# Transposing one head pair's features ahead of three others, in the one block that gets them from SBUF

## The chip, the cores and the metric

The kernel runs on one core of a Trainium2 chip. A core has five engines with queues of their own: TensorE (PE in the profile, with PEld for its weight loads), VectorE (DVE), ScalarE (ACT), GpSimd (POOL) and SyncE (SP, which issues the DMAs here). Each engine takes its instructions in the order in which they stand; between engines they wait for each other by semaphores. The metric is the device time of one execution in microseconds, as the median of several runs.

## The reference

Four sequences of 576 tokens, 8 heads of 64 features. The result of attention goes through a two-layer block with a squared ReLU.

```python
scores = scale * q @ k^T, causal;  a = softmax(scores);  local = a @ v
phi(x) = where(x > 0, x, exp(x) - 1) + 1
mem_out = (phi(q) @ M_prev) / (phi(q) @ z_prev + 1e-6)
g = sigmoid(beta);  attn = g * mem_out + (1 - g) * local      # per head
x = attn as [2304 tokens, 512]
out = relu(x @ w_in)^2 @ w_out                                # 512 -> 2048 -> 512
```

All inputs and the result are float32.

## The kernel before

*Tiling.* Heads are worked on in 4 pairs a sequence, each pair filling the 128 partitions. A sequence's first 64 tokens are computed in `first_tokens`, apart from the others; the remaining 512 tokens are four query tiles of 128. For the first two sequences a pair is done in two passes, tiles 1 and 2 of all pairs first and then tiles 3 and 4; for the last two, all four tiles at once. The two-layer block works on blocks of 256 tokens: block 0 holds the first 64 tokens of all four sequences, block 1 the tiles 1 and 2 of sequence 0, and so on to block 8.

*Attention.* `attention` loads the pair's `kd`, `qm` and `vv`, splits them into a high and a low part (`qh`, `ql` on L363 and L364, `kh`, `kl`; the low parts repair the precision of a faster kind of matmul), computes scores into a PSUM tile `sp` of two banks with one buffer (L466), lets DVE add the mask and take the row's extreme while it copies them to SBUF (L485), exponentiates on ACT (L505), makes two float16 parts `a`, transposes them by DMA (`aT`, L549) and multiplies with the split values `vs` (L570 to L575). `memx` holds the pair's part of the memory term (L443), to which the local term is added (L585); a tile pair's features are then written to the DRAM tensor `xd` (L596). One pair's are kept back: those of the last pair of sequence 0 for tiles 1 and 2, which go into the list `last` as the SBUF tile `memx`.

*The two-layer block.* `moe(n)` makes eight groups `up` (L653 to L655: 24 matmuls of 256 columns each), squares and splits them (`r`, `gh`, `gl`), and adds them into `oacc` (L643 to L645: 12 matmuls of 512 columns for each group). After its seventh group, `prefetch` fetches the next block's features: a load `xn` from `xd` (L617), transposes on PE into a PSUM tile `px` (L620, L622), a copy `xh` on ACT (L625) and the rest `xl` on DVE (L626), all twice, for 128 tokens each. `px` and `up` share two PSUM buffers. Block 1 alone gets the list `last` as `tail`: three quarters of its features are read from `xd`, and the last quarter is transposed straight from `memx`.

*What sets the order.* `merge` interleaves the steps of attention, of the weights' loading and of block 0 in program order. From that, the framework's scheduler makes each engine's queue when the kernel is built: it plays the program through with a timing model and takes, whenever an engine is free in it, the ready instruction that stands first. So moving one instruction can reorder what comes after it on all engines. PSUM has two buffers each for `up`, `oacc` and for the small tiles `av` (`acc`, `pm`, `vt`), and the two banks of `sp`.

Of the kernel before, what the change touches and what calls it, by code (L numbers as in the profile page):

```python
# [8 lines left out]
F32 = mybir.dt.float32  # L9
# [81 lines left out]
def fused_kernel(ctx: ExitStack, tc: tile.TileContext, t0_d, zt_d, kk_d, qv_d, beta, w_in, w_out, out):  # L91
    nc = tc.nc
# [8 lines left out]
    ident = identr.bitcast(F32)  # L101
# [508 lines left out]
    def prefetch(b, blk, tail=None):  # L610
        nk = NK if tail is None else NK - 1
        xh = mo.tile([P, NK, BLK], F32R, tag="xh", name="xh", bufs=2)
        xl = mo.tile([P, NK, BLK], F32R, tag="xl", name="xl", bufs=2)
        for t in range(2):
            r0 = QT[1 + 2 * blk + t][0]
            src = mo.tile([P, DM], F32R, tag="x", name="xn", bufs=XB)
            nc.sync.dma_start(src.bitcast(F32)[:, : nk * P], xd[b][r0 : r0 + P, : nk * P])  # L617
            px = ps.tile([P, NK, P], F32R, tag="up", name="px", bufs=2)
            for k in range(nk):
                nc.tensor.transpose(px[:, k], src[:, k * P : (k + 1) * P], identr)  # L620
            if tail is not None:
                nc.tensor.transpose(px.bitcast(F32)[:, nk], tail[:, t], ident)  # L622
            px = px.bitcast(F32)
            ts = slice(t * P, (t + 1) * P)
            nc.scalar.copy(xh[:, :, ts], px)  # L625
            nc.vector.tensor_tensor(out=xl[:, :, ts], in0=px, in1=xh[:, :, ts].bitcast(F32), op=ALU.subtract)  # L626
        return xh, xl

    def moe(n):
# [17 lines left out]
        for j in range(NF // 2):  # L647
# [23 lines left out]
            if j == PJ and n + 1 < NBLK:  # L671
                assert n > 0 or last
                xq.append(prefetch(*blocks[n + 1], *last))
                last.clear()
                yield
# [133 lines left out]
```

## Time and profile before

| | |
|---|---|
| median of 3 runs | 601.41 us (599.22 to 602.59) |
| the profiled execution | 599.29 us |
| its span, first to last instruction | 597.5 us |
| PE busy | 551.6 us (92%) |
| DVE busy | 412.5 us (69%) |
| ACT busy | 328.1 us (55%) |
| mean granted clock of TensorE | 0.983 |

PE's 92% is a mean: from 160 us to the end of attention at about 440 us it is busy nearly all the time beside a DVE that is busy too, and from there to the end it works alone. A matmul's length in the timeline overlaps that of the next; what one costs PE is the distance of two starts. An idle time in brackets behind an instruction is that of its engine just before it, with what ended it.

### The profile page before, as it was taken

How to read it: one execution, taken by the hardware profiler on the slowest of the kernel's cores; microseconds unless marked ns; L12 is line 12 of the kernel's file. 1: busy time of each engine (PE TensorE's matmuls, PEld its weight loads, DVE VectorE, ACT ScalarE, POOL GpSimd, SP SyncE). 2: the span in 40 equal slices, each digit the busy share in tenths (PEclk: the TensorE clock that was granted, in tenths of full speed). 3: DMA queues.
4: the chain of work that ended last, by engine and by line, in shares of the span. 5: the costliest groups of instructions: out<-in, count | busy, mean ns of one | idle time of the engine just before them, and what ended most of it. 6: DMA issues, size and time to landing. Idle time of an engine off the chain costs nothing.

```text
span 597.5 us, 11549 instructions
## 1 busy us (share of the span) xinstructions
PE 551.6 (92%) x4198; PEld 483.4 (81%) x4198; DVE 412.5 (69%) x1285; ACT 328.1 (55%) x747; POOL 171.6 (29%) x139
## 2 busy tenths in 40 slices
PE   2478998699999899999999999999999999999997
PEld 2356886497888788888888888998889999999996
DVE  5999898789879799898697898988985101101100
ACT  3699786476756576776566555573553222213212
POOL 2502122033433233322332334214333211221221
PEclk9977999999999999999999999999999999999999
DMA  8957746757646566575663547555344000100000
GB/s 278 412 200 277 234 141 124 148 136 177 139 119 123 153 149 170 144 185 156 124 132 80 157 122 147 135 149 140 47 101 131 29 1 35 37 1 18 20 0 36
DMA packets 127576, 76.28 MB, mean 128 GB/s; under 512 B 99360, under 2 KB 112672, under 8 KB 127520
## 3 DMA queue, kind: packets, MB, share of 16 engines
q1 hardware_dynamic: 127520, 75.55, 47.8%
q8 instruction: 33, 0.54, 0.4%
q14 instruction: 23, 0.19, 0.1%
HBM read 42.63 MB, written 8.78 MB: 86 GB/s over the span
## 4 chain that ended last, share of the span: by engine, by line
PE 48%; DVE 25%; DMA 11%; ACT 8%; issue 5%; SPq 2%; POOL 1%; ACTq 0%; DVEq 0%
PE up L653 7%; PE up L655 7%; PE up L654 7%; PE oacc L643 7%; PE oacc L645 7%; PE oacc L644 7%; DVE a L545 5%; DMA vv<-in_qv_dram 4%; PE sp L466 3%; DMA aT<-a 3%; ACT e L505 3%; DVE e L485 3%; DVE memx L585 3%; DVE raw L165 2%; DVE w L169 1%
## 5 line engine op out<-in xcount | busy, mean ns | idle before, releaser
L653 PE MATMUL up<-xh,w 128*128 128x256 f32 x576 | 167.2, 290 | 2.9 <-ACT aF L525 2.8
L654 PE MATMUL up<-xl,w 128*128 128x256 f32 x576 | 166.3, 289 | 0.0
L655 PE MATMUL up<-xh,w 128*128 128x256 f32 x576 | 166.2, 289 | 0.0
L668 POOL TENSOR_TENSOR gl<-r,gh 128x512 fp32r<-128x512 f32 x72 | 97.0, 1348 | 206.9 <-DVE gh L667 127.4
L653 PEld LDWEIGHTS up<-xh,w 128*128 128x128 f32 x576 | 111.9, 194 | 8.3 <-ACT aF L525 3.0
L643 PE MATMUL oacc<-w,gh 128*128 128x512 f32 x288 | 115.1, 400 | 0.3 <-DVE gh L667 0.3
L654 PEld LDWEIGHTS up<-xl,w 128*128 128x128 f32 x576 | 111.9, 194 | 3.2 <-issue 0.7
L644 PE MATMUL oacc<-w,gh 128*128 128x512 f32 x288 | 113.6, 394 | 0.0
L655 PEld LDWEIGHTS up<-xh,w 128*128 128x128 f32 x576 | 111.8, 194 | 1.5 <-issue 0.4
L505 ACT ACTIVATE e<-e,mx 128x320 f32<-128x320 f32 (+3 forms) x128 | 77.9, 609 | 62.9 <-DVE memx L585 33.0
L645 PE MATMUL oacc<-w,gl 128*128 128x512 f32 x288 | 109.1, 393 | 0.0
L659 ACT ACTIVATE r<-up 128x512 f32<-128x512 f32 x72 | 42.3, 588 | 115.9 <-PE up L655 103.9
L661 POOL TENSOR_TENSOR r<-r 128x512 f32<-128x512 f32 x40 | 49.1, 1229 | 153.3 <-ACT r L659 150.0
L667 DVE CAST gh<-r 128x512 fp32r<-128x512 f32 x40 | 16.9, 423 | 106.5 <-ACT r L663 102.8
L545 DVE SCALAR_TENSOR_TENSOR a<-e,a 128x128 f16<-128x128 f32 x120 | 75.7, 655 | 16.9 <-ACT a L543 16.7
L643 PEld LDWEIGHTS oacc<-w,gh 128*128 128x128 f32 x288 | 54.3, 189 | 9.5 <-DVE gh L667 0.5
L645 PEld LDWEIGHTS oacc<-w,gl 128*128 128x128 f32 x288 | 53.2, 188 | 10.3
L644 PEld LDWEIGHTS oacc<-w,gh 128*128 128x128 f32 x288 | 54.4, 189 | 8.5
L543 ACT ACTIVATE a<-e 128x128 f16<-128x128 f32 x120 | 55.8, 520 | 3.0 <-DMA aT<-a 2.1
L485 DVE CUSTOM_DVE_ANT_0 e<-sp,mask 128x320 f32<-128x320 f32 (+3 forms) x128 | 47.3, 414 | 0.3
L585 DVE SCALAR_TENSOR_TENSOR memx<-s,sm,memx 128x64 f32<-128x64 f32 x120 | 38.0, 357 | 1.4
L575 PE MATMUL acc<-vs,aT 128*128 128x128 f16 x308 | 36.9, 220 | 0.0
(127 smaller groups left out, 875.6 us busy)
## 6 DMA issues: line engine op xcount, KB each, us to landing
raw<-in_w_in_dram SPq DMA_DIRECT2D x11, 512.0 KB, 7.1
vv<-in_qv_dram SPq DMA_DIRECT2D x16, 320.0 KB, 3.3
raw<-in_w_out_dram SPq DMA_DIRECT2D x9, 512.0 KB, 7.2
kd<-in_kk_dram SPq DMA_DIRECT2D x16, 288.0 KB, 3.0
out_dram<-o SPq DMA_DIRECT2D x16, 256.0 KB, 2.0
xd<-memx SPq DMA_DIRECT2D x31, 128.0 KB, 1.9
xn<-xd SPq DMA_DIRECT2D x14, 256.0 KB, 2.7
qm<-in_qv_dram SPq DMA_DIRECT2D x8, 321.0 KB, 3.1
```

The lines of the kernel that those rows point to most:

```text
L485: nc.vector.tensor_tensor_reduce(out=e[:, h, ka:kb], in0=sps[:, h, cs], in1=mask[:, 448 - q0 + ka : 448 - q0 + kb], scale=-0.125, scalar=3 ...
L505: ex = nc.scalar.activation(e[:n, h, :ke], e[:n, h, :ke], AF.Exp, bias=bs, scale=-1.0, accum_out=sm[:n, h : h + 1])
L543: nc.scalar.mul(av[:, :, o0 : o0 + w], x, SC)
L545: nc.vector.scalar_tensor_tensor(out=av[:, :, o0 + w : o0 + 2 * w], in0=x, scalar=SC, in1=av[:, :, o0 : o0 + w], op0=ALU.mult, op1=ALU.sub ...
L585: nc.vector.scalar_tensor_tensor(out=xo, in0=s3[:n, h], scalar=sm[:n, h : h + 1], in1=xo, op0=ALU.mult, op1=ALU.add,)
L643: nc.tensor.matmul(acc[t], gh[:, u, ts], w_out_op(f, 0), start=f == 0, stop=False)
L644: nc.tensor.matmul(acc[t], gh[:, u, ts], w_out_op(f, 1), start=False, stop=False)
L645: nc.tensor.matmul(acc[t], gl[:, u, ts], w_out_op(f, 0), start=False, stop=f == NF - 1)
L653: nc.tensor.matmul(up[:, u, :], w_in_op(f, k, 0), xh[:, k, :], start=k == 0, stop=False)
L654: nc.tensor.matmul(up[:, u, :], w_in_op(f, k, 0), xl[:, k, :], start=False, stop=False)
L655: nc.tensor.matmul(up[:, u, :], w_in_op(f, k, 1), xh[:, k, :], start=False, stop=k == NK - 1)
L668: nc.gpsimd.tensor_tensor(out=gl, in0=r, in1=gh.bitcast(F32), op=ALU.subtract)
```

## The change

In `prefetch`, the transpose of the tail's quarter stands ahead of the loop over the quarters from `xd`, not behind it. Only block 1 has a tail, so only there do instructions trade places in the program.

```diff
             px = ps.tile([P, NK, P], F32R, tag="up", name="px", bufs=2)
+            if tail is not None:
+                nc.tensor.transpose(px.bitcast(F32)[:, nk], tail[:, t], ident)
             for k in range(nk):
                 nc.tensor.transpose(px[:, k], src[:, k * P : (k + 1) * P], identr)
-            if tail is not None:
-                nc.tensor.transpose(px.bitcast(F32)[:, nk], tail[:, t], ident)
```

The line numbers trade places too: the tail's transpose is L622 before and L620 after, the loop's L620 before and L622 after. Scheduled anew, PE's queue differs from the 321st to about the 3,100th of some 4,390 rows, and the other engines' queues over the same stretch; the matmuls are the same.

PE, at block 1's transposes: `xn` is the load from `xd`, `memx` the tail; `pm` is the memory term and `sp` the scores of two attention pairs, `up` block 0's last group. The six transposes of `xn` stood earlier, behind scores of 512 columns and behind a run of `acc` matmuls:

```order
 L403 LDWEIGHTS vx
 L403 MATMUL vt<-identb,vx 128x128
-L622 MATMUL px<-identr,memx 128x128
 L434 MATMUL pm<-qm,pe 128x130 x2
-L622 MATMUL px<-identr,memx 128x128
+L620 MATMUL px<-identr,memx 128x128
+L622 MATMUL px<-identr,xn 128x128 x3
+L620 MATMUL px<-identr,memx 128x128
+L622 MATMUL px<-identr,xn 128x128 x3
 L466 MATMUL sp<-kd,qm 128x512 x2
 L653 MATMUL up<-xh,w_1003 128x256
```

All eight transposes now stand in one place. On DVE the two splits on L626, which stood as the first and fourth row behind the reading of the scores, stand as the fifth and the seventh now.

SP, between two loads of attention, some 25 us later in the program: `o` is block 0's output, `qm` the queries of the next pair, `vv` its values. Before:

```order
L596 DMA xd_91<-memx 128x2x128
L688 DMA out_dram<-o 64x512 x4
L340 DMA qm<-in_qv_dram 128x130
L340 DMA qm<-in_qv_dram 128x256
L343 DMA vv<-in_qv_dram 128x640
```

And now:

```order
L596 DMA xd_91<-memx 128x2x128
L340 DMA qm<-in_qv_dram 128x130
L340 DMA qm<-in_qv_dram 128x256
L688 DMA out_dram<-o 64x512 x4
L343 DMA vv<-in_qv_dram 128x640
```

The queries have passed the four stores. PE, at the scores that are made of these queries (`kh` to `ql`). Before, they stood in the middle of an `up` group, behind 12 matmuls of `oacc`:

```order
L654 MATMUL up<-xl,w_109 128x256
L655 MATMUL up<-xh,w_109 128x256
L466 MATMUL sp<-kh,qh 128x448 x2
L466 MATMUL sp<-kh,ql 128x448 x2
L466 MATMUL sp<-kl,qh 128x448 x2
```

And now, inside the run of `acc` matmuls ahead of those:

```order
L572 MATMUL acc<-vs,aT 128x64
L466 MATMUL sp<-kh,qh 128x448 x2
L466 MATMUL sp<-kh,ql 128x448 x2
L466 MATMUL sp<-kl,qh 128x448 x2
L466 MATMUL sp<-kh,qh 128x64 x2
L466 MATMUL sp<-kh,ql 128x64 x2
L466 MATMUL sp<-kl,qh 128x64 x2
L575 LDWEIGHTS aT
L575 MATMUL acc<-vs,aT 128x128
L643 MATMUL oacc<-w_102,gh 128x512
```

The scores have passed 12 matmuls of `oacc` and 10 of `up`; the next two groups of scores moved forward about as far, and those behind them stand within two microseconds of their old place in PE's work.

## Rows read from the trace of the kernel before

**Rows 1.** The page's forty slices of PE (tenths), and its chain by engine.

```profile
PE   2478998699999899999999999999999999999997
...
PE 48%; DVE 25%; DMA 11%; ACT 8%; issue 5%; SPq 2%; POOL 1%; ACTq 0%; DVEq 0%
```

**Rows 2.** Windows: us, then each engine's busy us; granted clock, DMA share, GB/s.

```profile
100.00:120.00 20.00, 14.29 (x81) 9.89 (x80) 15.54 (x57) 10.46 (x22) 2.49 (x3) 0.92 0.62 143
120.00:160.00 40.00, 38.75 (x338) 34.30 (x337) 35.88 (x117) 28.25 (x67) 16.46 (x13) 1.00 0.67 151
160.00:440.00 280.00, 272.66 (x2259) 239.34 (x2257) 243.04 (x787) 172.05 (x413) 89.52 (x70) 1.00 0.56 135
```

**Rows 3.** PE's waits, 100 to 230 us, then after 230: total, times, longest.

```profile
PE sp L466 <- DVE mx L485: 5.2, 3, 3.0
PE sp L466 <- DVE ql L364: 3.2, 3, 1.3
...
PE acc L570 <- DVE memx L443: 3.0, 4, 1.0
```

**Rows 4.** Timeline of PE: start us, length us, instruction, idle time before it.

```profile
104.77 0.43 PE L620 MATMUL px<-identr,xn 128*128 128x128 f32 x3 [0.48 <-DMA xn<-xd]
...
110.81 1.19 PE L466 MATMUL sp<-kd,qm 64*128 64x448 f32 x8 [1.82 <-DVE mx L485]
...
116.22 1.42 PE L466 MATMUL sp<-kd,qm 64*128 64x512 f32 x4 [3.04 <-DVE mx L485]
117.57 0.58 PE L653 MATMUL up<-xh,w 128*128 128x256 f32 x1
...
120.56 0.28 PE L655 MATMUL up<-xh,w 128*128 128x256 f32 x1
120.68 0.28 PE L653 MATMUL up<-xh,w 128*128 128x256 f32 x1
```

**Rows 5.** Timeline of DVE around the two splits on L626.

```profile
116.08 0.69 DVE L626 TENSOR_TENSOR xl<-px,xh 128x512 fp32r<-128x512 f32 x1
...
116.75 0.17 DVE L441 RECIPROCAL nm<-nm 128x4 f32<-128x4 f32 x1
...
117.48 0.41 DVE L443 TENSOR_TENSOR memx<-pm,nm 128x256 f32<-128x256 f32 x1
```

**Rows 6.** Timeline of ACT: the second copy of the features.

```profile
115.83 0.56 ACT L625 CAST xh<-px 128x512 fp32r<-128x512 f32 x1
```

**Rows 7.** Windows of 1 us; the granted clock follows POOL's busy time.

```profile
118.00:119.00 1.00, 1.00 (x6) 1.00 (x6) 1.00 (x3) 0.85 (x2) 0.00 (x0) 0.50 1.27 295
...
121.00:122.00 1.00, 1.00 (x11) 1.00 (x10) 1.00 (x5) 0.45 (x2) 0.00 (x0) 1.00 0.03 12
```

**Rows 8.** Timeline of SP's queue: start us, time that its issues took.

```profile
130.91 0.38 SPq L596 DMA_DIRECT2D xd<-memx  x1
133.22 3.95 SPq L688 DMA_DIRECT2D out_dram<-o  x4
137.27 1.02 SPq L340 DMA_DIRECT2D qm<-in_qv_dram  x2
```

**Rows 9.** Timeline of DVE, 128 to 180 us, around `ql` on L364.

```profile
136.14 0.74 DVE L485 CUSTOM_DVE_ANT_0 e<-sp,mask,mx 128x512 f32<-128x512 f32 x1
...
141.35 0.42 DVE L364 TENSOR_TENSOR ql<-qm,qh 128x256 fp32r<-128x256 f32 x1 [0.58 <-ACT qh L363]
...
146.89 0.22 DVE L485 CUSTOM_DVE_ANT_0 e<-sp,mask 128x64 f32<-128x64 f32 x1
```

**Rows 10.** Timeline of PE, 129 to 158 us, around the next pair's scores.

```profile
136.43 0.40 PE L645 MATMUL oacc<-w,gl 128*128 128x512 f32 x1
136.66 0.40 PE L643 MATMUL oacc<-w,gh 128*128 128x512 f32 x1
...
141.92 0.47 PE L466 MATMUL sp<-kh,qh 64*128 64x448 f32 x2 [0.93 <-DVE ql L364]
...
148.70 0.53 PE L466 MATMUL sp<-kh,qh 64*128 64x512 f32 x2
```

## The prediction

> **What bounds the kernel now.** I read the page's forty slices first, then its chain, then PE's waits, and last the order of the instructions at the places that moved. From the fifth slice on PE is at nine tenths nearly everywhere, and 48% of the chain that ended last is PE's own work, 25% VectorE's (DVE) [rows 1]. So PE is the engine to watch: with the same matmuls, the time moves by what PE's idle time and its clock do. The windows say how much there is to move [rows 2]. From 100 to 120 us PE works 14.29 us of 20, from 120 to 160 us 38.75 of 40, from 160 to 440 us 272.66 of 280. That is 5.7, 1.25 and 7.3 us of idleness, 14.3 in all, and it lies in the part whose order the change touches: block 1's features are transposed at about 105 to 113 us, and PE's two queues read alike again some 3,100 rows in, at about 400 us. What ends these waits is mostly DVE. From 100 to 230 us PE waited 5.2 us for the scores' buffer (the readers on L485) and 3.2 us for `ql` (L364) [rows 3]; after 230 us the largest entry is 3.0 us for a buffer that L443 frees. The stretch at 100 to 120 us is a DVE-bound knot: DVE works 15.54 us there although it stands still for a load at its start.
>
> **The change, part by part.**
>
> *The transposes themselves.* The same eight are done. Before, six stood early, three of them at 104.77 us after 0.48 us of waiting for the load `xn` [rows 4], and only the two of the tail came late. Now all eight stand behind the tail's features, between the 448-column scores and the 512-column scores. Three take 0.43 us, so six are at most 0.9 us. Their new place is followed by a wait of 3.04 us (scores at 116.22, released by DVE) and their old one by a wait of 1.82 us (scores at 110.81, also released by DVE) [rows 4]. DVE's queue up to both releases is row for row the same in both orders. So the early work ends up to 1.3 us sooner and waits longer, the late work ends up to 0.9 us later and waits less, and scores start at 110.81 and 116.22 as before. Term: 0. If the second cover were gone it would cost the 0.9 us.
>
> *The copies out of PSUM.* DVE's first split (L626) started at 116.08 us, the second two small steps later [rows 5]. Now the first stands behind four small steps of attention: three of one to four columns, of about the 0.17 us that one of them shows, and L443 of 0.41 us. At most it ends at 116.08 + 0.51 + 0.41 + 0.69 = 117.69 us. Who waits: block 0's last `up` group, which needs the first PSUM buffer back and began at 117.57 us, behind the scores [rows 4]. So 0 to 0.12 us; I take 0. ScalarE now copies both halves from 115.83 us on [rows 6], where it copied the second half before; that is early enough for the splits. Block 1's own first group starts 24 matmuls after 117.57 us and does not see the second split.
>
> *The clock.* The granted clock was 0.50 from 118 to 119 us and back at 1.00 from 121 to 122 us [rows 7], after the 3.04 us of idleness. From 117.57 to 120.56 us 15 matmuls of `up` began, the first and last of them in the rows; their 14 distances would be 1.7 us at the 0.12 us between the last two rows, which stand at full clock [rows 4]. The low stretch cost 3.0 - 1.7 = 1.3 us. With the early transposes and their wait gone (0.48 and some 0.7 us), the first idle gap grows from 1.82 to about 3.0 us, and the second shrinks from 3.04 to about 2.3 us. Bounds: 1.3 us won, if the low stretch goes or falls where PE waits for DVE anyway; 1.3 us lost, if it lasts twice as long. I take 0: the two gaps together stay about as long, and one of them is as long as the one that the low stretch followed.
>
> The Trainium skill ("TensorE: Matmul & The Clock Gate", "HAM oscillation") says that the array restarts at the low rate after each long gap, again and again. The trace agrees for the 3.04 us gap, and shows none after the 1.82 us one. By that rule the lengthened first gap could bring a low stretch of its own, and the sum would be 1.3 us higher.
>
> *The next pair's scores.* On SP the two loads of `qm` are now issued ahead of the four stores of block 0's output, where they stood behind them. Before, SP finished the store to `xd` begun at 130.91 us, began the outputs at 133.22 and `qm` only at 137.27 us [rows 8]. `ql` came at 141.35 us, 4.1 us behind that issue [rows 9], and the 448-column scores, which need it, were late by 0.93 us at 141.92 [rows 10]. Issued after the store at about 131.3 us, `qm` would give a `ql` at 135.4 us, if DVE were free. It is not: `ql` now stands behind the reading of the 512-column scores, whose second half began at 136.14 and lasted 0.74 us [rows 9]; that makes 137.2 us. PE comes to these scores sooner too. They are moved ahead of 12 matmuls of `oacc` at 0.23 us (the distance of two neighbours [rows 10]) and 10 of `up` at 0.12 us, 4.0 us together, so PE stands there at 141.92 - 0.93 - 4.0 = 137.0 us. The wait shrinks from 0.93 to about 0.3 us: a gain of 0.6 us. The store of the output is what is late next, by some 1 us, and nobody in attention waits for it but `vv`, the load queued behind it.
>
> *The two groups of scores after it* also stand about 4 us earlier in PE's work, while DVE's work ahead of their releases shrinks by only 1 to 2 us. At 148.70 us the next scores had slack: the last reading before them, begun at 146.89 us, ended at 147.1 [rows 9, 10]. That is 1.6 us. With PE 4.3 us earlier (3.7 of order, 0.6 of the wait that went) and DVE 2 us earlier (1.4 of order, and the 0.58 us that it stood before `ql` [rows 9]), 1.6 - 4.3 + 2.0 = -0.7: a wait of up to 0.7 us. I take 0.3 here and 0.3 for the group behind, 0.6 in all. Bounds: nothing, or, if DVE isn't earlier at all, the full 4.0 us that PE was brought forward. I stay near the low end because DVE's work up to these releases is itself shortened.
>
> *The rest, to 440 us.* Scores stand within 2 us of their old place in PE's work, now a little later, and what doesn't depend on PE stays. Of the 7.3 us of waits [rows 2] some will go and others come. No row gives a sign; bounds from the same row are half of it won (3.7 us) and half as much again lost (3.7 us). I take 0.
>
> Sum: 0 + 0 + 0 - 0.6 + 0.6 + 0 = 0. The profiled execution took 599.3 us (span 597.5, 1.8 outside), so it would be 599.3 again; the median of the runs is 2.1 us above it, so I forecast **601.4 us**. Own range of this case: 599 to 603.5.
>
> **Rivals.**
>
> *A queue that stands (slower).* PE takes its instructions in order, so scores that come 4.0 us earlier and find `ql` no earlier hold up 12 `oacc` and 10 `up` matmuls that could have run. For it: DVE is busy 35.88 of 40 us from 120 to 160 us [rows 2], so pulling its customers forward does not make it faster, and `vv` still queues behind the output. Against it: `qm` is issued some 6 us earlier. If `qm`'s lead is eaten (by its buffer, or by DVE's queue), PE waits the full 4.0 us once; it gets little back, since it has only short waits later to lose. 601.4 + 4.0 = 605.4 us. It decides once the new wait at these scores passes 3 us.
>
> *The waits shrink (faster).* From 160 us on the scores stand later in PE's work relative to DVE's than before, by 1 to 3 us at most groups up to about 270 us. If that takes the waits for `ql` (3.2 us, of which 0.93 are counted above [rows 3, 10], leaves 2.3) and half of the 3.0 us for L443's buffer, 1.5 us, it is 3.8 us: 597.6 us. For it: these waits are just the kind that such an order shortens. Against it: `ql` waits on a load, and loads are held by SP's order, not by DVE's work alone.
>
> *A second low stretch of the clock* as above: 602.7 us, which is still no change.
>
> That the change doesn't do what it says is out: the order shows the tail's transposes first.
>
> **How the numbers follow.** Two times closer than 0.5%, 3.0 us here, can't be told apart. The forecast has 0.46, the second low stretch 0.09, the queue that stands 0.20, the shrinking waits 0.25. The first two are "within 0.5%": 0.55. Faster is 0.25, slower 0.20. The range must reach into both outer cases, so from 597.4 (just past the shrinking waits) to 605.0 (short of the whole 4.0 us): it leaves out the half of the slow case beyond it and the tails.
>
> **What would show it.** In the changed profile: scores still released by DVE near 110.8 and 116.2 us with PE idle ahead of both (term 1); the clock at 0.50 for 3 to 4 us once near 117 us; `ql` of the third split pair at about 137 us instead of 141.35 and a wait under 0.5 us ahead of its scores; PE's idle sum from 120 to 440 us within 3 us of 8.6. If that sum is above 11.5 us, with the waits at scores between 135 and 160 us, the queue that stands was right; if below 5.5 us, the shrinking waits. A wait for `xn` or for L626 of over 0.5 us on PE would refute the first two parts.

## The result and the profile after

The changed kernel takes 608.38 us (median of 4 runs, 607.59 to 609.72) where the kernel before takes 601.65 us beside it: ratio 1.012, 95% interval 1.0084 to 1.0157. Timed a second time it took 606.94 us, ratio 1.0086 (1.0054 to 1.0119). So it is slower by 5 to 7 us; the forecast was 601.4 us and its range ended at 605.0. The profiled execution took 609.03 us, with a span of 607.2.

The same lines as in [rows 1], of the changed kernel: PE's forty slices, and the chain by engine.

```profile
PE   2586999698999999799999999899999999999997
...
DVE 36%; PE 35%; DMA 11%; ACT 10%; issue 6%; SPq 1%; POOL 1%; ACTq 0%; DVEq 0%
```

PE's share of the chain fell from 48% to 35%, VectorE's (DVE's) rose from 25% to 36%. DMA's share stayed at 11%, ScalarE's went from 8% to 10%. A new dent stands in slice 17 (243 to 258 us). The windows that answer to [rows 2]:

```profile
100.00:120.00 20.00, 14.89 (x76) 9.85 (x75) 14.50 (x55) 10.19 (x24) 3.10 (x3) 0.78 0.59 121
120.00:160.00 40.00, 38.02 (x325) 33.63 (x326) 36.15 (x107) 26.45 (x60) 14.45 (x11) 0.98 0.66 154
160.00:440.00 280.00, 267.65 (x2188) 235.06 (x2187) 240.50 (x775) 170.35 (x409) 87.83 (x69) 0.99 0.57 132
```

PE's idleness is 2.0 us from 120 to 160 us and 12.35 us from 160 to 440 us: 14.3 us, where it was 1.25 + 7.3 = 8.6 us. The second profile of the same kernel has 12.1 us. PE's waits from 230 to 440 us, which answer to the last line of [rows 3]:

```profile
PE acc L570 <- DVE memx L443: 2.9, 4, 0.9
PE sp L466 <- DVE ql L364: 2.5, 3, 1.8
PE acc L570 <- DVE vs L416: 2.1, 1, 2.1
```

The first was there before (3.0 us). The other two are new at this size: before, `ql` had 0.5 us there in two waits, and `vs` none. Now the transposes. PE's timeline at the two scores of [rows 4], and two of the windows of 1 us that answer to [rows 7] (the granted clock is the third number from the end):

```profile
112.36 2.18 PE L466 MATMUL sp<-kd,qm 64*128 64x448 f32 x8 [3.83 <-DVE mx L485]
117.77 2.08 PE L466 MATMUL sp<-kd,qm 64*128 64x512 f32 x4 [0.90 <-DVE mx L485]
```

```profile
112.00:113.00 1.00, 0.64 (x2) 0.50 (x4) 0.96 (x5) 1.00 (x3) 0.00 (x0) 0.50 0.00 0
...
122.00:123.00 1.00, 1.00 (x10) 1.00 (x10) 1.00 (x5) 1.00 (x3) 0.00 (x0) 1.00 0.19 65
```

The first gap grew from 1.82 to 3.83 us, the second shrank from 3.04 to 0.90 us, and the two scores stand 5.41 us apart, to the hundredth what they did before (110.81 to 116.22). The clock fell to 0.50 (1.2 GHz) near the end of the longer gap, at 111.2 us, and stayed there for 10.2 us, the short gap included; in the kernel before it was low for 3.4 us, from 116.9 us. So the transposes ran at half clock, inside a stretch that DVE sets.

Then the next pair's loads, which answer to [rows 8 to 10]: SP's queue, then `ql` on DVE, then the scores on PE.

```profile
131.51 0.38 SPq L596 DMA_DIRECT2D xd<-memx  x1
133.83 0.80 SPq L340 DMA_DIRECT2D qm<-in_qv_dram  x2
136.29 2.46 SPq L688 DMA_DIRECT2D out_dram<-o  x4
...
139.50 0.42 DVE L364 TENSOR_TENSOR ql<-qm,qh 128x256 fp32r<-128x256 f32 x1
...
140.07 0.47 PE L466 MATMUL sp<-kh,qh 64*128 64x448 f32 x2 [0.86 <-DVE ql L364]
```

`ql` comes 1.85 us earlier than before, but PE comes earlier too, and the wait is 0.86 us where it was 0.93. What holds `qm` up on SP, from 131 to 135 us:

```profile
SPq L340 <- PE pm L434: 1.9, 1, 1.9
```

That matmul reads an earlier pair's `qm`: the load's buffer, one of two, was not free.

Last, the place where most is lost. This is the chain of waits of the changed kernel (start us, length us, what) around 240 us:

```profile
240.95 0.03 DVE vz L409
240.98 0.90 issue
...
243.28 2.02 DVE vs L416 x2
245.30 0.02 SPq L343
...
245.35 2.94 DMA vv<-in_qv_dram
...
251.17 1.26 DVE memx L585 x2
252.43 0.35 DVE ql L364
...
252.82 1.13 PE sp L466 x12
```

There is no PE in this chain from 222 to 252.8 us: DVE's small steps, a store to `xd`, and the loads `qm` and `vv` follow each other. In the kernel before, the chain runs through PE from 232.3 to 241.1 us. SP's queue, the changed kernel first:

```profile
225.67 0.57 SPq L596 DMA_DIRECT2D xd<-memx  x1
228.03 0.33 SPq L617 DMA_DIRECT2D xn<-xd  x1
228.45 0.86 SPq L340 DMA_DIRECT2D qm<-in_qv_dram  x2
...
240.68 0.38 SPq L596 DMA_DIRECT2D xd<-memx  x1
245.35 0.33 SPq L343 DMA_DIRECT2D vv<-in_qv_dram  x1
245.78 0.86 SPq L340 DMA_DIRECT2D qm<-in_qv_dram  x2
```

and the kernel before, the second pair:

```profile
234.14 0.54 SPq L596 DMA_DIRECT2D xd<-memx  x1
234.77 0.94 SPq L340 DMA_DIRECT2D qm<-in_qv_dram  x2
237.60 0.33 SPq L343 DMA_DIRECT2D vv<-in_qv_dram  x1
```

Now `qm` is issued behind `vv`, and `vv` can't go before L416 has read its buffer (245.30 us); `qm` goes out 11 us later than before. PE's two long waits at the end of it:

```profile
244.88 0.22 PE L570 MATMUL acc<-vs,aT 128*128 128x128 f16 x1 [2.13 <-DVE vs L416]
252.82 0.47 PE L466 MATMUL sp<-kh,qh 64*128 64x448 f32 x2 [1.85 <-DVE ql L364]
```

### The profile page after: what moved, and what is told of

Read it like the earlier page. It is cut to its first block, busy times and chain, and to the rows that moved or that the text cites. A ratio compares the mean times of both kernels' runs of the same rounds, so it can differ in the third digit from the quotient of the medians.

```text
span 607.2 us, 11549 instructions
## 1 busy us (share of the span) xinstructions
PE 555.1 (91%) x4198; PEld 485.8 (80%) x4198; DVE 417.3 (69%) x1285; ACT 327.6 (54%) x747; POOL 171.4 (28%) x139
## 4 chain that ended last, share of the span: by engine, by line
DVE 36%; PE 35%; DMA 11%; ACT 10%; issue 6%; SPq 1%; POOL 1%; ACTq 0%; DVEq 0%
DVE a L545 8%; PE up L653 5%; PE up L654 5%; PE up L655 5%; DVE e L485 5%; PE oacc L643 5%; PE oacc L645 5%; PE oacc L644 5%; ACT e L505 5%; DMA vv<-in_qv_dram 4%; DVE memx L585 3%; DVE vs L416 2%; ACT a L543 2%; DMA aT<-a 2%; DVE raw L165 2%
## 5 line engine op out<-in xcount | busy, mean ns | idle before, releaser
L668 POOL TENSOR_TENSOR gl<-r,gh 128x512 fp32r<-128x512 f32 x72 | 97.4, 1353 | 218.0 <-DVE gh L667 127.5
L659 ACT ACTIVATE r<-up 128x512 f32<-128x512 f32 x72 | 42.4, 589 | 121.5 <-PE up L655 110.7
L545 DVE SCALAR_TENSOR_TENSOR a<-e,a 128x128 f16<-128x128 f32 x120 | 77.0, 661 | 23.4 <-ACT a L543 22.8
L661 POOL TENSOR_TENSOR r<-r 128x512 f32<-128x512 f32 x40 | 47.8, 1194 | 143.8 <-ACT r L659 138.1
L543 ACT ACTIVATE a<-e 128x128 f16<-128x128 f32 x120 | 55.9, 521 | 4.0 <-DMA aT<-a 3.7
```

Source lines behind the costliest of these rows:

```text
L543: nc.scalar.mul(av[:, :, o0 : o0 + w], x, SC)
L545: nc.vector.scalar_tensor_tensor(out=av[:, :, o0 + w : o0 + 2 * w], in0=x, scalar=SC, in1=av[:, :, o0 : o0 + w], op0=ALU.mult, op1=ALU.sub ...
L668: nc.gpsimd.tensor_tensor(out=gl, in0=r, in1=gh.bitcast(F32), op=ALU.subtract)
```

## The experiments

Theory 1: the loss comes from the new order behind the transposes, since the scheduler plans all five queues anew. Theory 2: it comes from the moved transposes (one long gap, a low clock). To take them apart, the queues were held to a given order. At the end of the program's construction each instruction is tied behind the one that is to stand ahead of it on its engine; the tie sets an order and adds no wait. The traces bear this out: before_qm, held to the old order but for two loads, has the rows of the kernel before on every engine but SP, and its time (ratio 1.0005).

```diff
+    pin(tc, nc)
...
+def pin(tc, nc):
...
+    for engine, text in ROWS.items():
...
+        for a, b in zip(rows, rows[1:]):
+            tc.add_manual_dep(b, a.name, AFTER, reason="row by row")
```

`ROWS` is, for each engine, the list of its instructions in the wanted order. Orders can be joined at a place where both have issued the same instructions on an engine. The runs, 5 to 12 executions each (dve_act_window 4) beside 11 to 21 of the kernel before:

| run | held to | us | before | ratio (95%) |
|---|---|---|---|---|
| local_only | changed to 118 us, old behind | 602.03 | 601.26 | 1.0019 (0.9994 to 1.0044) |
| rest_only | old to 118 us, changed behind | 606.19 | 601.26 | 1.0097 (1.0073 to 1.0121) |
| after_sp_before | changed, SP's queue old | 610.31 | 601.26 | 1.0156 (1.0125 to 1.0186) |
| before_sp_after | old, SP's queue changed | 613.45 | 601.26 | 1.0193 (1.0170 to 1.0216) |
| qm_first | changed, `qm` ahead of `vv` twice | 606.40 | 601.49 | 1.0087 (1.0058 to 1.0116) |
| new_till_240 | changed to 240 us, old behind | 609.39 | 601.49 | 1.0129 (1.0090 to 1.0167) |
| new_from_240 | old to 240 us, changed behind | 608.33 | 601.49 | 1.0108 (1.0075 to 1.0142) |
| after_again | the changed kernel | 606.94 | 601.49 | 1.0086 (1.0054 to 1.0119) |
| window_old | changed, all old at 197 to 258 us | 604.79 | 600.40 | 1.0069 (1.0041 to 1.0096) |
| vs_first | as qm_first, `vs` earlier | 606.07 | 600.40 | 1.0104 (1.0070 to 1.0137) |
| before_qm | old, `qm` ahead of stores once | 600.99 | 600.40 | 1.0005 (0.9983 to 1.0028) |
| tail_at_1 | (planned anew) | 613.08 | 600.40 | 1.0206 (1.0168 to 1.0243) |
| sp_window | changed, SP old at 197 to 258 us | 608.12 | 600.88 | 1.0099 (1.0062 to 1.0136) |
| dve_act_window | changed, DVE and ACT old there | 622.67 | 600.88 | 1.0358 (1.0328 to 1.0387) |
| pe_window | changed, PE old there | 625.73 | 600.88 | 1.0394 (1.0356 to 1.0432) |
| before_sp_window | old, SP changed there | 607.66 | 600.88 | 1.0113 (1.0080 to 1.0146) |
| tail_first_0 | (planned anew) | 606.71 | 600.52 | 1.0105 (1.0075 to 1.0134) |
| before_qm3 | old, `qm` ahead at three places | 600.02 | 600.52 | 1.0002 (0.9983 to 1.0021) |

To place the loss, I took the start of the same scores on PE in two traces and followed the lag behind the kernel before. Ahead of anything that moved, at 84 us, the lag already lies between -0.8 and +4.0 us, differing with each execution; so only its growth is read. Two pairs of rows as an example, the first two of before, the others of after:

```profile
222.74 0.53 PE L466 MATMUL sp<-kh,qh 64*128 64x512 f32 x2
...
257.01 0.41 PE L466 MATMUL sp<-kh,qh 64*128 64x320 f32 x2 [0.28 <-DVE ql L364]
```

```profile
226.30 0.50 PE L466 MATMUL sp<-kh,qh 64*128 64x512 f32 x2
...
265.25 0.41 PE L466 MATMUL sp<-kh,qh 64*128 64x320 f32 x2
```

The lag is 3.56 us at the first scores and 8.24 us at the second: a growth of 4.7 us. All growths, in us:

| stretch (us, in before) | after | after_again | tail_first_0 | rest_only | window_old | local_only |
|---|---|---|---|---|---|---|
| 103 to 223 | +3.0 | +2.8 | +2.5 | +0.6 | +3.2 | +0.4 |
| 223 to 257 | +4.7 | +3.7 | +4.7 | +3.4 | +1.6 | +0.7 |
| 257 to 379 | 0.0 | +0.9 | -1.3 | -0.6 | -0.2 | +1.1 |
| 379 to 389 | +1.5 | +1.4 | +1.5 | +1.5 | +0.7 | 0.0 |

Behind 389 us nothing is added. Each trace is of one execution. Those of before, local_only and rest_only lie 2.1, 2.9 and 2.3 us below the medians of their kernels, those of after, after_again and window_old 0.7, 1.8 and 2.7 us above. So the sums of the columns are not the differences of the medians, and local_only and rest_only look better in this table than they are.

**The change alone, and the rest alone.** The cut is the first place behind the transposes at which both orders agree.

> All five queues stand as in the changed kernel up to the 512-column scores behind the eight transposes (117.8 us in its trace), and from there on as in the kernel before. Theory 1 (the loss comes from the new order of what follows): 601.7 to 603.5 us, since the scores of the changed kernel were only 1.6 us late at 110.8 us and 2.3 us at 125 us, of which the low clock took some. Theory 2 (the moved transposes themselves, by one longer gap and a low clock three times as long): most of the 6.7 us, so 606 to 608.4 us.

> The other half: the transposes and all that stands ahead of the 512-column scores as in the kernel before, everything behind them as in the changed kernel. Theory 1: 605.5 to 608 us, with the waits of 2.13 and 1.85 us near 245 and 253 us and the late scores from 388 us on again. Theory 2: 600.5 to 603 us.

Theory 1 held on both sides: the moved transposes with the old order behind them cost 0.8 us (interval -0.4 to +2.6), the new order without them 4.9 us (4.4 to 7.3 by the ratio). Together that is 5.7 us, about what the whole change costs (5.5 and 6.7 us in its two rounds). The local part looks as the prediction had it. PE's timeline of local_only (its lines are numbered 24 higher):

```profile
108.34 1.98 PE L490 MATMUL sp<-kd,qm 64*128 64x448 f32 x8 [3.07 <-DVE mx L509]
113.75 1.13 PE L490 MATMUL sp<-kd,qm 64*128 64x512 f32 x4 [1.32 <-DVE mx L509]
```

One gap grew to 3.07 us, the other shrank, and the scores are again 5.41 us apart: DVE's reading sets both ends, as before.

**One queue alone.** Is SP's order the cause?

> The changed kernel with one queue, SyncE's, in the order of the kernel before; PE, DVE, ScalarE and GpSimd stay in the changed order. Theory 1 in its narrow form (the loads are issued in a worse order: vv ahead of qm, and vv holds the queue until its buffer is free): 603 to 605 us, the wait for ql near 252 us gone. Theory 1 in its wide form (PE's and DVE's own order): 607 to 609 us. Theory 2: 608 us.

> The kernel before with SyncE's queue alone in the order of the changed kernel. Narrow form of theory 1: 604 to 606 us, with a wait for ql of more than 1.5 us near 245 us. Wide form and theory 2: 601 to 602.5 us.

Both were worse than expected by any theory: SP's old queue under the changed order loses another 2 to 4 us (the intervals touch), and its changed queue under the old order 12 us. In after_sp_before the scores fall back by 7.4 us against the trace of after between those at 132 and 149 us; in before_sp_after they fall back by 7.6 us against before between 209 and 245 us and by 5 us between 282 and 291 us. A queue of loads is good or bad only with the order that uses them.

**The loads `qm` ahead of `vv`.** On SP, at two places:

```diff
 L596 DMA xd_92<-memx 128x2x128
-L343 DMA vv<-in_qv_dram 128x640
 L340 DMA qm<-in_qv_dram 128x130
 L340 DMA qm<-in_qv_dram 128x256
+L343 DMA vv<-in_qv_dram 128x640
```

> The changed kernel with two edits in SyncE's queue alone: at the two places where vv is issued ahead of the two loads of qm (the pairs whose first scores stand at 206 us and at 253 us in its trace), vv comes behind them. If vv, which has to wait for its buffer, holds qm and so ql up (the loads of the second pair went out at 245.8 us, in the kernel before at 234.8 us), the wait of 1.85 us for ql near 252 us goes and 2 to 4 us are won back: 604 to 606 us. If PE would be late there anyway, by the matmuls that the new order puts ahead, or for the 2.13 us wait for vs just before: within 1 us of the changed kernel, 607.5 to 609 us.

606.40 us, just outside the first expectation, below the second, and not told apart from the changed kernel (606.94 us beside it). `qm` went out at 238.84 us, and the wait for `ql` fell from 1.85 to 0.51 us, but the wait for `vs` stayed, 2.32 us:

```profile
242.31 0.22 PE L570 MATMUL acc<-vs,aT 128*128 128x128 f16 x1 [2.32 <-DVE vs L416]
250.41 0.47 PE L466 MATMUL sp<-kh,qh 64*128 64x448 f32 x2 [0.51 <-DVE ql L364]
```

**One half of the program, the changed kernel again.**

> All queues in the changed order up to about 240 us (behind the scores sp_2644 on PE), in the order of before from there on. If the loss sits in one stretch behind 240 us: 602 to 604 us, the lag at 237.8 us in the changed kernel's trace having been 2.1 us. If it is a debt built up earlier that only comes due there: 606 us or more.

> The opposite: the order of before up to about 240 us, the changed order behind it. One bad stretch behind 240 us: 605 to 608 us, with waits for vs and ql near 245 to 253 us again. A debt from earlier: 601 to 602.5 us.

> The changed kernel once more, profiled a second time, for the clock: its first trace had a low stretch of 10.2 us at 111 to 122 us and another of 3.4 us at 255 us, where a kernel with the same order up to 118 us had 3.4 us and none. If the clock follows the order, the two low stretches come again; if it is a matter of the single execution, they don't, and the median stays near 608 us (607 to 609.5) all the same.

Either half of the changed order costs about as much as the whole (7.9 and 6.8 us). In new_till_240 the lag still grows by 3.8 us from 223 to 257 us and by another 3.8 us from 282 to 291 us, where the changed kernel loses nothing; in new_from_240 it grows by 1.0 us up to 223 us and by 5.7 us from 223 to 257 us. So these two halves don't add up, and these two runs don't settle where a debt is made.

The clock of the second profile fell for 3.4 us at 112 us, as in before, but then for another 6.8 us from 139 us:

```profile
140.00:142.00 2.00, 2.00 (x16) 1.89 (x15) 1.73 (x4) 2.00 (x5) 1.10 (x1) 0.50 0.78 214
142.00:144.00 2.00, 2.00 (x7) 1.29 (x7) 1.92 (x6) 1.18 (x3) 1.27 (x1) 0.50 1.03 230
```

So the place differs with the execution, and the sum hardly does: from 100 to 150 us it is 10.2 us at half clock in after and in after_again, and in 7 of the 9 other traces that have the changed order up to there (6.8 us in qm_first, and 13.0 us in after_sp_before, where SP's queue is the old one). In before, local_only and rest_only it is 3.4 us, and at most 6.8 us in the other traces of the old order. The mean clocks of all executions say the same: 0.976 in the 11 of the changed kernel, 0.982 in the 78 of before and in rest_only, 0.981 in local_only. A mean of 0.976 is what a span has that runs at 0.50 for 4.8% of its length: 28 to 29 us in the changed kernel, against 22 in before, 21 in rest_only and 23 in local_only, the start of the kernel included. What such a stretch costs can be read in after_again, where PE is busy through it: between the scores at 142 and 149 us the lag grows by 3.1 us, where it grows by 0.4 us in after and 0.3 us in tail_first_0 at full clock.

The other low stretch came again: the mean clock from 240 to 260 us is 0.91 in after, after_again, tail_first_0, qm_first and vs_first, and 1.00 in before, rest_only, window_old and sp_window. In after the lag grows by 1.5 us between the scores at 245 and 251 us, over this stretch; in rest_only by nothing.

**All queues old in one stretch.** Cuts at which all engines agree lie near 197 and 258 us.

> The changed order, except that all five queues stand as in the kernel before in one stretch, from about 197 to 258 us; the orders agree at both ends of it, engine by engine, in what has been issued. If the 5 us that the changed order loses between the scores at 237.8 and 257.0 us come from the order in that stretch: 602 to 604 us. If they are a debt from ahead of it (PE running ahead of a VectorE that is no earlier): 606 to 609 us, the lag growing by 4 to 5 us in the stretch as before.

The time is 604.79 us, 4.4 us above before, between the two expectations; its interval overlaps those of the changed kernel. Where it works, the trace shows: the lag grows by 1.6 us from 223 to 257 us, not by 3.7 to 4.7. The window from 240 to 260 us of before, after and window_old, in this order:

```profile
240.00:260.00 20.00, 19.57 (x176) 16.54 (x173) 19.44 (x56) 15.19 (x33) 6.43 (x5) 1.00 0.59 139
```

```profile
240.00:260.00 20.00, 16.03 (x127) 14.25 (x127) 18.96 (x59) 13.62 (x30) 5.03 (x4) 0.91 0.60 144
```

```profile
240.00:260.00 20.00, 19.72 (x159) 16.86 (x159) 17.90 (x67) 13.91 (x31) 5.67 (x5) 1.00 0.66 153
```

PE stands idle for 4.0 us of it in after, and for 0.3 us in window_old (for 0.4 and 1.2 us of the 20 us ahead of it).

**`vs` earlier on DVE and ScalarE**, on top of qm_first (DVE's queue is shown; ScalarE's L414 moves ahead of one L659 and two L543):

```diff
 L409 TENSOR_SCALAR vz<-gs,vy 128x2
+L416 SCALAR_TENSOR_TENSOR vs<-vv,vy,vs 128x5x64 x2
 L545 SCALAR_TENSOR_TENSOR a<-e,a 128x2x64
 L550 SCALAR_TENSOR_TENSOR sm<-sm,vz 128x2 x2
 L554 RECIPROCAL sm<-sm 128x2 x2
 L545 SCALAR_TENSOR_TENSOR a<-e,a 128x2x384
-L416 SCALAR_TENSOR_TENSOR vs<-vv,vy,vs 128x5x64 x2
```

> The kernel with qm ahead of vv, and near 240 us also the two halves of vs (L416) on VectorE moved ahead of the two splits of a (L545) and the four small steps behind them, with ScalarE's half of vs (L414) moved ahead of three of its instructions, as the kernel before has it. The wait of 2.3 us of the products (L570) for vs at 242.3 us should go down to about 1 us or less. If that wait is what is lost there: 604 to 605.3 us, 1.3 us and more below qm ahead of vv alone (606.4 us). If VectorE's work as a whole is late there: another wait takes its place within 10 us, and the time stays at 606 to 607 us.

The second expectation held. The wait for `vs` is gone, and others stand in its place, 2.8 us for 2.8:

```profile
246.88 0.50 PE L645 MATMUL oacc<-w,gl 128*128 128x512 f32 x1 [0.83 <-POOL gl L668]
252.21 0.67 PE L466 MATMUL sp<-kh,qh 64*128 64x448 f32 x2 [1.95 <-DVE ql L364]
```

**One queue old in that stretch.**

> The changed order, except that SyncE's queue alone stands as in the kernel before from about 197 to 258 us (26 issues: qm ahead of the load xn that waits for the store xd, qm ahead of vv). If the loads of that stretch are what loses the 5 us there (the chain of waits of the changed kernel runs through xd, xn, qm and vv from 225 to 252 us): 602.5 to 604.5 us, the wait for ql near 252 us under 0.5 us. If VectorE's order is: 605.5 to 608 us, as with qm ahead of vv alone.

> The changed order, except that VectorE's and ScalarE's queues stand as in the kernel before from about 197 to 258 us. If their order loses the 5 us there: 602.5 to 604.5 us, the wait for vs near 245 us under 0.5 us. If the loads do: 605.5 to 608 us with a wait for ql of 1 us or more.

> The changed order, except that PE's queue alone stands as in the kernel before from about 197 to 258 us. If PE merely stands ahead of a VectorE that sets the pace there, its own order makes no difference: 605.5 to 608 us. If the scores brought forward in PE's queue are what starts the late chain: 602.5 to 604.5 us.

> The kernel before with SyncE's queue alone in the changed order from about 197 to 258 us. If those 26 issues lose the 5 us by themselves: 604 to 606.5 us, the lag growing between the scores at 230 and 257 us. If only all queues together do: 600.5 to 602.5 us.

No queue is the culprit by itself. SP's old order there wins nothing (608.12 us), its new order costs the old kernel 6.8 us, and the others cost 14 us and more beyond the changed kernel. PE's longest entries from 180 to 275 us, for sp_window, dve_act_window and pe_window in this order:

```profile
PE sp L466 <- DVE ql L364: 3.2, 3, 2.0
```

```profile
PE oacc L643 <- ACT gh L665: 7.9, 3, 3.5
```

```profile
PE acc L570 <- DVE s L577: 6.9, 2, 3.8
```

A queue out of step with the others waits for them, each time for something else.

**Other small edits.** tail_at_1 puts the tail's transpose second; tail_first_0 moves it first in the first half only:

```diff
             for k in range(nk):
+                if tail is not None and k == 1:
+                    nc.tensor.transpose(px.bitcast(F32)[:, nk], tail[:, t], ident)
                 nc.tensor.transpose(px[:, k], src[:, k * P : (k + 1) * P], identr)
```

```diff
+            if tail is not None and t == 0:
+                nc.tensor.transpose(px.bitcast(F32)[:, nk], tail[:, t], ident)
...
+            if tail is not None and t != 0:
```

> Neither order: the tail's features are transposed second, behind the first of the three quarters, and the scheduler plans all the rest anew. The queues differ from those of both kernels over some 1,400 rows of PE's. If the loss belongs to the particular order of the changed kernel: any time, 600 to 603 us as likely as 606. If nearly any re-planned order loses against the one of before, through waits of PE for VectorE spread over 100 to 400 us: 604 to 609 us.

> Half of the change: only for the first 128 rows are the tail's features transposed first; for the second 128 rows the three quarters from DRAM come first, as before. The scheduler then plans all queues as in the changed kernel, row for row but for the second half's four transposes. If the plan is what costs: the whole loss, 606 to 608.5 us. If the moved transposes cost: about half of it, 603 to 605 us.

tail_at_1 is a third plan and slower still, 12.7 us. tail_first_0 has the changed kernel's plan, row for row but for four transposes, and its loss, 6.2 us, not half of it. So the plan costs it, and two new plans of two are worse than the old one.

**`qm` ahead of stores in the old order.** Once, then at three places:

```diff
 L596 DMA xd_91<-memx 128x2x128
+L340 DMA qm<-in_qv_dram 128x130
+L340 DMA qm<-in_qv_dram 128x256
 L688 DMA out_dram<-o 64x512 x4
-L340 DMA qm<-in_qv_dram 128x130
-L340 DMA qm<-in_qv_dram 128x256
```

> The kernel before with one edit: the two loads of qm of the third split pair stand ahead of the four stores of block 0's output in SyncE's queue, as in the changed kernel, and nothing else moves. The prediction's term for this (ql 4 us earlier, the wait of 0.93 us at 141.92 us gone): 600.3 to 601 us, 0.4 to 1 us below the kernel before. Theory 1, by which a queue that is moved alone is out of step with the others: 601.5 to 603 us.

> The kernel before with the loads of qm moved ahead in SyncE's queue at three places, past stores alone (and one kd): ahead of the four stores of block 0's output, ahead of a store to xd and a kd, and ahead of a store to xd and two of the output. The scores' waits for ql behind them were 0.93, 1.03 and 1.29 us at 141.92, 189.18 and 202.39 us. If they go and nothing takes their place: 598 to 599.5 us, 1.5 to 3 us below the kernel before. If SyncE's queue can't be moved without the others: 601 to 604 us.

The wait at the third split pair's scores (split: made of `kh`, `kl`, `qh` and `ql`) fell from 0.93 to 0.25 us in before_qm, and to 0.26 us in before_qm3. There the wait of 1.03 us fell to 0.20 us too, and that of 1.29 us is gone, but PE waits 1.16 us for DVE's L577 just behind those scores, at 204.75 us. The times don't show a gain: 1.0005 (0.9983 to 1.0028) and 1.0002 (0.9983 to 1.0021). A gain up to 1 us isn't excluded, the expected 1.5 to 3 us are. No order tried beats the old one. SP's largest wait in before_qm from 133 to 138 us:

```profile
SPq L340 <- PE pm L434: 2.4, 1, 2.4
```

`qm` goes out at 136.76 us, 2.9 us behind the start of the store at 133.87 us, not at once: as in the changed kernel, its buffer isn't free earlier.

## Why the prediction was wrong

- *The transposes, 0, and the copies, 0.* Right: local_only costs 0.8 us, with 0 inside its interval. Scores were released by DVE at both places, the same distance apart, and PE waited neither for `xn` nor for L626.
- *The clock, 0, bounds 1.3 us.* The shape was right: the first gap became the long one (3.07 to 3.83 us for the forecast 3.0), the second 0.9 to 1.9 us for 2.3, and the low stretch moved to the longer one. The size was not: the changed order has 10.2 us at half clock from 100 to 150 us, three times as much as before, in one piece or in two, and the bound was twice as long. One such piece cost about 2.7 us where it met a busy PE (after_again, 142 to 149 us). By the rule quoted from the Trainium skill ("TensorE: Matmul & The Clock Gate", "HAM oscillation") a second low stretch would come with a second long gap. Second low stretches came, but the trace agrees only in part, since no long gap stands ahead of them: from 139.1 us in after_again behind waits of 1.00 and 0.36 us, near 255 us in after behind waits of 2.13 and 1.85 us. rest_only, with 2.31 and 1.73 us there, has none, so the length of a gap alone doesn't decide it.
- *The next pair's scores, -0.6.* The wait went from 0.93 only to 0.86 us. Two inputs were off. `qm` couldn't be issued at 131.3 us; it went at 133.83, held for 1.9 us by its buffer, as the first rival feared. And `ql` stands behind DVE's readings, at 139.50 us: the 137.2 us of the text plus the 2 us by which all stood later. Alone, in the old order, the edit does shorten the wait to 0.25 us.
- *The two groups of scores after it, +0.6.* 0.33 us was waited at the scores at 152.90 us, nothing at those at 147.15 us. The size was about right.
- *The rest, to 440 us: 0, bounds 3.7 us on either side.* This is the step that failed. PE's idleness from 120 to 440 us went from 8.6 to 14.3 us, 12.1 in the second trace, and rest_only, which is this term with the two before it and without the transposes, costs 4.9 us. I took the re-planned order to be as good as the old one, and made the bounds symmetric. What the runs showed in its place: 3.4 to 4.7 us are lost from 223 to 257 us, where the chain leaves PE for DVE and the loads that wait for DVE, and 1.5 us from 379 to 389 us, by waits of PE of 0.40, 0.49 and 0.92 us for DVE. And the bounds were not symmetric: there were 8.6 us of idleness to win at the most, much of it for data that is late in any order, while an order out of step loses 7 to 25 us.
- *The rivals.* "A queue that stands" had the sign and 605.4 us, but not the place: the waits from 135 to 160 us are 0.42, 0.37, 0.86 and 0.33 us, none near the 3 us from which it should decide. Its general reason held 90 us further on. "The waits shrink" is out: the waits for `ql` (3.2 and 0.5 us before) are 3.1 and 2.5 us.

What stays open: the traces of the changed plan lose 2.5 to 3.0 us up to 223 us, those of local_only and rest_only 0.4 and 0.6 us. The 6.8 us more at half clock, which only the former have, go with the difference and could pay for it, but no run holds the clock, so this is read and not tested; and the medians of the two parts add up to the whole without it. Open too is what in the plan makes it worse: the repairs of single waits (qm_first, vs_first) moved the wait on, and giving all five queues their old order in the worst stretch won it back in the trace but only about 2 us, within the intervals, in the time.

## What to carry to other kernels

When a scheduler plans the whole program, price a moved instruction by how far the plan changes, not by the instruction: compare the orders engine by engine, and where they differ over hundreds of microseconds in a kernel with little idleness left, there is more to lose than to gain (here two new plans of two lost). To test such a change, hold the queues to one order and move the part alone; it tells the edit from the plan in two runs. Don't repair single queues of a plan: a shorter wait in one place was paid back in the next, and kernels with one queue or two in another plan's order were 7 to 25 us slower than the old one. And take the clock from more than one profile: the place of its low stretch differed, its sum hardly did.

## What the runs showed of the hardware

Some of DVE's instructions take longer beside one of GpSimd's. The halves of `vs` in before alone, then in after beside L668 on GpSimd (POOL):

```profile
236.52 1.01 DVE L416 SCALAR_TENSOR_TENSOR vs<-vv,vy,vs 128x320 f16<-128x320 f32 x2
```

```profile
243.06 1.42 POOL L668 TENSOR_TENSOR gl<-r,gh 128x512 fp32r<-128x512 f32 x1 [1.12 <-ACT gh L665]
...
243.28 2.02 DVE L416 SCALAR_TENSOR_TENSOR vs<-vv,vy,vs 128x320 f16<-128x320 f32 x2
```

Two take 1.01 us alone and 2.02 us there. The Trainium skill ("SBUF — State Buffer", "Who interferes with whom") says that the two engines share a port pair, and that of two operations that both need it the one issued first holds it to its end while the other is blocked. The trace agrees: L409, 0.22 us long with no GpSimd beside it, took 1.02 us from 240.95 us in after, and GpSimd's L661, begun 0.04 us before it, ended at 241.95 us. It works the other way too: where a split of 1024 columns on L545 had begun first (290.85 us in after), it kept its 1.20 us and GpSimd's L668, begun just behind it, took 2.21 us, where the mean of all 72 is 1.35 us. Of these splits in the two traces, the only three of 1.9 us had begun 0.2 to 0.5 us behind an operation of GpSimd's; one that began 0.14 us behind such an operation, on the heels of another split, kept its 1.22 us.

Summed over 100 to 440 us (each instruction's length less that of its like with no GpSimd beside it, where that is over 0.1 us; an estimate), DVE loses 35 to 36 us in before, 36 to 39 us in the two traces of after and 40 to 41 us in rest_only. So it isn't what tells the plans apart as a whole. From 223 to 257 us it is about 3 us in before and about 5 us in after: some 2 us more of DVE's time, in the stretch where DVE sets the pace. How much of the loss there comes from it, no run shows.
